# An RWKV-6 recurrence and a gated FFT convolution in one kernel: zero matmuls early on TensorE, the bonus added on VectorE, shared buffers, spectrum products slot by slot, and a new instruction order

## The chip, the cores and the metric

The kernel runs on one core of a Trainium2 chip. The metric is device time in microseconds of one execution, as the median of three runs. Engines are called as in the profile: PE is TensorE (PEld its weight loads), DVE is VectorE, ACT is ScalarE, POOL is GpSimd and SP is SyncE, which issues most of the DMAs.

## What is computed

Two layers. The first is a recurrence over 768 steps for 4 batches of 8 heads of 48 channels; the second projects the result three ways, convolves one projection along the sequence with a filter by FFT, multiplies by the other two and projects out.

```python
for t in range(S):
    cur = np.einsum('bhd,bhe->bhde', u[None] * kt, vt)
    y[:, :, t] = np.einsum('bhd,bhde->bhe', rt, state + cur)
    state = wt[:, :, :, None] * state + np.einsum('bhd,bhe->bhde', kt, vt)
...
x = attn_out.transpose(0, 2, 1, 3).reshape(B, S, H * D)
x1, x2, x3 = np.split(x @ w_proj, 3, axis=-1)
x2_conv = np.fft.irfft(np.fft.rfft(x2, axis=1) * np.fft.rfft(filter_fft, axis=0), axis=1)
return (x1 * x2_conv * x3) @ w_out
```

The term with `u` is the bonus: at each step it adds v times a number per head, the sum of r, k and u over the channels.

## The kernel before

**First layer.** The sequence of each batch is cut in 6 chunks of 128 steps, 24 chunks in all, numbered through the batches. A chunk is one set of [128 steps x 384 channels] tiles, and goes through these steps, whose names are those of the order table:

- `ldw ldk ldr ldv` (L384): four loads of 192 KB from a layout with 192-byte rows, each kind into a ring of 5 buffers.
- `lw` (ACT, L390) takes the logarithm of w; `cs`, `ce` (PE, L394 to L406) form its running sums; `en`, `eq`, `ph` (ACT, L412 to L424) their exponentials.
- `kh`, `q` (L430, L433) scale k and r by them, `rk`, `rku`, `cc` (L436 to L442) make the bonus number of each head, `v` (L231 to L233) casts v, and `vc` (L448) multiplies v by the bonus. They run on DVE or POOL, as the table says.
- `tqk` (PE, L454) transposes scaled k and r, `tT` copies them out of PSUM, `sc` (PE, L467) makes the scores, `mt` (DVE, L474) masks them, `kv` (PE, L483, L485) and `S` (DVE, L492) carry the state on.
- `y` (PE, L499 to L507) adds up in PSUM: vc through an identity matrix, then state times r, then scores times v. `xn` copies it out, `yt` (PE, L518) transposes it, `xT` copies that; for the second half of a batch `sa`, `sb` (DVE, L526, L529) form sums and differences with the first half.

**Second layer**, for each batch: `x2` (PE, L562) projects sums and differences, `ab` copies out; `f` (PE, L348, L356) is the forward transform in six slots of 128 rows, `X` copies out; `ua ub uc ud` (L584) multiply the spectrum by the filter's, `pr`, `pi` (L589, L593) combine the products; `iE`, `iO` (PE, L602) are the inverse transform in two halves for each of three column blocks, `ec`, `s`, `d` (L229 or L231, L617, L622) put them together. `p1`, `p3` (PE, L539) are the other two projections, `x1` copies one out, `g` (DVE, L555) multiplies them, `yy` (DVE, L627) multiplies by the convolution. `po` (PE, L634) projects out, `o` copies to a tile and `st` (L643) stores it. The filter's own spectrum (`fs fd hf H hg`) is made from one load, `ldfilt` (L307), and the transform matrices from sines (`ang`, `sin`, `m2t`, `m2c`).

**What sets the order.** A table of words written out by hand, `ORDER`, gives the order of the program. `V:ua.1.0` is: on DVE, ua of batch 1, piece 0; `P:y5@3` is: on PE, y of chunk 5, into PSUM bank 3. Each engine executes its own words in this order and waits in line for its inputs and buffers; nothing is reordered, on SP's DMA queue either. Six PSUM banks are shared by all steps and one wide tile is for the scores.

**What the steps of the prediction touch.** `GRAN = (3, 3, 3, 1)` says how many slots a spectrum product takes at once: in batches 0 to 2 one instruction covers all three pairs of slots (128x1152), in batch 3 there are three of 128x384. Tiles x1, ab, X, U and y exist once; the output tile exists twice, the second one in the filter's bytes. Before the table starts, PE runs 8 matmuls on a tile of zeros (`hot<-warm`, L687).

Of the kernel before, what the change touches and what calls it, by code (L numbers as in the profile page):

```python
# [12 lines left out]
INT32 = mybir.dt.int32  # L13
# [17 lines left out]
WARM = 8  # L31

# [4 lines left out]
A:tLn0 S:ldu G:masks S:ldw1 S:ldk0 S:ldw0 G:iota S:ldw2 S:ldk2 V:ang2 S:ldk1 V:ang0 S:ldw3  # L37
V:ang1 S:ldv1 A:lw2 A:lw0 P:cs2@0 P:ce2@1 S:ldr1 P:ce0@2 A:eq2 A:lw1 S:ldr0 P:ce1@3 P:cs1@4
P:cs0@5 A:eq1 S:ldr2 A:eq0 A:en1 S:ldv0 A:en0 V:kh1 A:ph2 A:lw3 G:kh0 A:en2 S:ldk3 A:v1 V:kh2
A:ph0 A:sin S:ldw5 V:q0 V:rk0 P:tqk0@4 S:ldw6 V:q1 G:q2 V:tT0 S:ldv2 V:rku0 G:v0 P:tqk2@5 V:cc0  # L40
P:cs3@1 S:ldr3 V:rk2 P:kv0@0 G:vc0 P:sc0@8 V:S0 P:ce3@2 V:mt0 S:ldw4 G:rku2 A:tT2 G:rk1 S:ldv3
V:cc2 P:y0@4 A:lw5 P:sc2@8 A:eq3 V:xn0 P:tqk1@0 A:en3 S:ldk4 V:rku1 G:v2 A:ph1 P:yt0@5 P:cs5@4
V:cc1 P:kv1@1 A:xT0 V:mt2 S:ldk6 A:lw6 G:rk3 A:ph3 A:tT1 S:ldr4 V:S1 G:vc2 A:lw4 V:vc1 P:kv2@3
A:en5 G:q3 S:ldv4 P:sc1@8 V:kh3 P:cs6@5 P:cs4@2 P:ce6@0 A:en4 G:rku3 P:y2@1 S:ldw8 V:S2 P:ce5@4
V:xn2 A:eq5 S:ldr5 G:v3 A:eq6 V:mt1 P:yt2@2 G:kh4 P:ce4@3 A:ph6 P:tqk3@1 S:ldr6 A:eq4 V:cc3
G:rk4 A:xT2 P:y1@4 V:tT3 S:ldk5 A:xn1 V:q4 G:rku4 P:sc3@8 P:m2t3@0 S:ldw7 P:m2t0@2 V:mt3
P:tqk4@1 P:yt1@4 A:tT4 S:ldr8 V:m2c3a G:q5 V:cc4 A:en6 V:vc3 P:m2t5@1 S:ldv7 P:sc4@8 A:xT1 G:rk6
# [88 lines left out]
def kernel(  # L136
# [307 lines left out]
    def op_v(e, c):  # L444
        copy(e, v_b[c % 4], ld["v"][c % 5])
# [274 lines left out]
```

## Time and profile before

| | |
|---|---|
| runs | 188.52 us median of 3 (187.33 to 189.53) |
| profiled execution | 188.97 us, span of its instructions 186.7 us |
| busy: PE, DVE, ACT, POOL | 154.7, 159.5, 117.3, 107.4 us |
| mean granted clock of PE | 0.962 |
| first logarithm starts | 7.92 us |
| filter load issued | 93.54 us |
| last input loads issued | 107.02 to 109.75 us |
| PE clock granted in 40 to 50 us | 0.65 |

The span is the time from the first to the last instruction of the profiled execution; the rest of its time lies around it. A row of a group names the line, the engine, the operation, output<-input with their shapes and the count, then busy time in all and the mean in ns of one, then the idle time of that engine just ahead of the group and what ended it. A row of a timeline starts with start and length in us. The rows of stages give start and length, then busy us and (count) of PE, PEld, DVE, ACT and POOL, the granted clock, the share of the DMA engines' time and GB/s.

### The profile page before, as it was taken

The page shows a single profiled execution, that of the slowest core. Times are in us where ns is not written, and L with a number is a line of the kernel's source. Part 1 is how long each engine was busy: PE and PEld are TensorE (multiplying, and loading weights), DVE is VectorE, ACT ScalarE, POOL GpSimd, SP SyncE. Part 2 cuts the span into 40 slices and gives each one's busy share as a digit, 9 for nine tenths or more (in the row PEclk, how much of TensorE's full clock was granted, in tenths as well). Part 3 has the DMA queues.
Part 4 walks back from the last instruction along what each step waited for, and adds up shares of the span by engine and source line. Part 5 has one row for each costly group of instructions (what it writes and reads, how often), then busy time and mean ns, then how long its engine had stood idle before and what let it go on. Part 6 is the DMA issues. An engine that isn't in the chain of part 4 may idle for free.

```text
span 186.7 us, 4118 instructions
## 1 busy us (share of the span) xinstructions
PE 154.7 (83%) x1526; PEld 97.8 (52%) x1526; DVE 159.5 (85%) x302; ACT 117.3 (63%) x257; POOL 107.4 (57%) x120
## 2 busy tenths in 40 slices
PE   5147787665799988897977799999999999999971
PEld 2115456444666546563655555756556655556630
DVE  6829989786989799989998979999998999699760
ACT  2289756976585497697486969988356415531532
POOL 6024899398651482995995636636651866781000
PEclk9999999995589999999999969999999999999999
DMA  4999999999999983999999890400001000335336
GB/s 104 202 219 201 192 188 205 199 177 197 193 195 188 213 172 76 196 191 214 176 248 241 172 203 5 63 4 0 0 4 42 0 0 4 126 125 214 130 144 235
DMA packets 105043, 26.41 MB, mean 141 GB/s; under 512 B 100288, under 2 KB 104640, under 8 KB 105024
## 3 DMA queue, kind: packets, MB, share of 16 engines
q1 hardware_dynamic: 104224, 24.98, 61.0%
q0 software_dynamic: 800, 1.18, 3.8%
q8 instruction: 12, 0.20, 0.4%
q14 instruction: 7, 0.06, 0.1%
HBM read 22.61 MB, written 4.72 MB: 146 GB/s over the span
## 4 chain that ended last, share of the span: by engine, by line
PE 56%; DVE 24%; ACT 9%; issue 4%; DMA 3%; SPq 2%; ACTq 0%
PE p L539 10%; PE po L634 6%; DVE mt L474 5%; PE iE L602 4%; PE iO L602 4%; PE f L356 4%; PE x L562 4%; ACT qkT L229 3%; PE tqk L454 3%; PE sc L467 3%; DVE cc L442 3%; PE y L507 2%; DVE S L492 2%; PE f L348 2%; DVE rku L439 2%
## 5 line engine op out<-in xcount | busy, mean ns | idle before, releaser
L539 PE MATMUL p<-xT,wproj 128*128 128x384 bf16 x144 | 30.0, 330 | 2.3 <-DVE S L492 2.0
L474 DVE TENSOR_TENSOR mt<-sc,mask_excl 128x1024 bf16<-128x1024 f32 x24 | 29.1, 1214 | 2.2 <-PE sc L467 2.2
L448 POOL TENSOR_TENSOR vc<-v,cc 128x384 bf16<-128x384 bf16 x19 | 16.8, 887 | 18.0 <-DVE cc L442 6.3
L430 POOL TENSOR_TENSOR qk<-ldk,en 128x384 bf16<-128x384 f32 x15 | 16.0, 1068 | 17.3 <-ACT phi L424 9.0
L436 POOL TENSOR_TENSOR rk<-ldr,ldk 128x384 bf16<-128x384 f32 x18 | 20.1, 1118 | 6.7 <-DVE rku L439 5.6
L229 ACT ACTIVATE qkT<-tqk 128x1024 bf16<-128x1024 bf16 x19 | 19.5, 1029 | 6.2 <-PE tqk L454 6.0
L454 PE MATMUL tqk<-ident,qk 128*128 128x128 bf16 x192 | 16.8, 238 | 5.0 <-POOL qk L430 2.1
L539 PEld LDWEIGHTS <-wproj 128*128 128x128 bf16 x144 | 13.0, 98 | 11.5 <-issue 4.4
L433 POOL TENSOR_TENSOR qk<-ldr,eq 128x384 bf16<-128x384 f32 x13 | 14.1, 1085 | 7.2 <-ACT eq L418 4.8
L229 ACT ACTIVATE x<-p 128x384 bf16<-128x384 f32 x20 | 9.6, 492 | 12.9 <-PE p L539 10.2
L454 PEld LDWEIGHTS <-qk 128*128 128x128 bf16 x192 | 13.2, 106 | 8.1 <-issue 4.0
L390 ACT ACTIVATE lg<-ldw 128x384 bf16<-128x384 f32 x24 | 12.7, 532 | 6.0 <-DMA ldw<-in_w_dram 5.9
L634 PE MATMUL po<-wout,y 128*128 128x384 bf16 x72 | 14.3, 326 | 1.3 <-DVE y L627 1.1
L412 ACT ACTIVATE en<-cs 128x384 f32<-128x384 f32 x24 | 11.7, 496 | 5.3 <-PE cs L394 5.2
L562 PE MATMUL x<-wproj,sd 128*128 128x384 bf16 x72 | 14.8, 326 | 0.0
L555 DVE TENSOR_TENSOR g<-p,x 128x384 bf16<-128x384 f32 x24 | 13.0, 549 | 1.8 <-PE p L539 1.8
L394 PE MATMUL cs<-lg,mask_incl 128*128 128x384 bf16 x24 | 9.5, 413 | 5.3 <-ACT lg L390 4.6
L418 ACT ACTIVATE eq<-ce 128x384 f32<-128x384 f32 x24 | 11.7, 495 | 3.1 <-PE ce L406 1.7
L492 DVE TENSOR_TENSOR S<-kv,phi 128x384 bf16<-128x384 f32 x20 | 11.0, 550 | 2.7 <-PE kv L485 2.2
L442 DVE TENSOR_REDUCE cc<-rku 128x8 f32<-128x384 bf16 x24 | 12.9, 541 | 0.1
L229 ACT ACTIVATE xn<-y 128x384 bf16<-128x384 f32 x17 | 8.4, 494 | 6.7 <-PE y L507 6.6
L602 PEld LDWEIGHTS <-P 128*128 128x128 bf16 x96 | 9.3, 98 | 6.1
(133 smaller groups left out, 410.2 us busy)
## 6 DMA issues: line engine op xcount, KB each, us to landing
ldw<-in_w_dram SPq DMA_DIRECT2D x24, 192.0 KB, 3.9
ldk<-in_k_dram SPq DMA_DIRECT2D x24, 192.0 KB, 3.8
ldv<-in_v_dram SPq DMA_DIRECT2D x24, 192.0 KB, 4.0
ldr<-in_r_dram SPq DMA_DIRECT2D x24, 192.0 KB, 3.9
out_dram<-o SPq DMA_DIRECT2D x12, 192.0 KB, 2.0
out_dram<-filt SPq DMA_DIRECT2D x12, 192.0 KB, 2.0
filt<-in_moe_filter_fft_dram SPq DMA_DIRECT2D x1, 1152.0 KB, 7.4
wproj<-in_moe_w_proj_dram POOLq DMA_DIRECT2D x1, 864.0 KB, 8.7
```

What stands on the lines that cost most here:

```text
L229: nc.scalar.activation(out=o, in_=i, func=AF.Copy)
L430: two(e).tensor_mul(qk_b[c % 3][:, 1, :, 0:D], ld["k"][c % 5], en_b[c % 3])
L436: two(e).tensor_mul(rk_b[c % 2], ld["r"][c % 5], ld["k"][c % 5])
L442: nc.vector.tensor_reduce(out=cc_b[c % 3], in_=rku_b[c % 2], axis=AX.X, op=ALU.add)
L448: two(e).tensor_mul(vc_b[c % 3], v_b[c % 4], cc_b[c % 3].to_broadcast([L, H, D]))
L454: nc.tensor.transpose(p[:, x, j, :], qk_b[c % 3][:, x, 2 * j:2 * j + 2, :], ident)
L474: nc.vector.tensor_mul(mt_b[c % 3], bank_of[f"sc{c}"].rearrange("p q j t -> p (q j) t"), dataclasses.replace(m[:, :], ap=[m[:, :].ap[0], [ ...
L492: nc.vector.tensor_mul(S_b[nth(c)], bank_of[f"kv{c}"], ph_b[nth(c)].to_broadcast([L, HP, 2, D]))
L539: nc.tensor.matmul(p, wproj[:, cb, col0:col0 + L], xT_b[b % 2][:, cb, sl], start=(cb == 0), stop=(cb == CB - 1),)
L562: nc.tensor.matmul(p, sd_b[q][0][:, cb, ti * L:(ti + 1) * L], wproj[:, cb, C:2 * C], start=(cb == 0), stop=(cb == CB - 1),)
L602: nc.tensor.matmul(p, P_b[q % 2][b % 2][:, q // 2, cb * L:(cb + 1) * L], m, start=(n == 0), stop=(n == len(slots) - 1),)
L634: nc.tensor.matmul(p, y_b[0][:, cb, ti * L:(ti + 1) * L], wout[:, cb, :], start=(cb == 0), stop=(cb == CB - 1),)
```

## The change

Five things, and all of them in one step.

1. **Zeros.** A word of PE can end in `+n`: then n matmuls of the zero tile go into the PSUM tile of that word just ahead of it. They write 384 columns at most, and the word's own first matmul overwrites them. The table has 78 in twelve places: 69 of them belong to chunks 0 to 5 (11 ahead of ce0, 6 ahead of tqk0, 11 ahead of y2, and so on), 9 stand ahead of the first output product of batch 3.
2. **Bonus.** y no longer gets vc through the identity matrix (24 matmuls fewer). `xn` becomes an addition of PSUM and vc, on DVE in all 24 chunks; before, it was a copy, 17 times on ACT and 7 times on DVE.
3. **Buffers.** Load rings go from 5 to 6, x1, ab, X and y from 1 to 2. The angles lie in the output tile's bytes, U in the filter's, the index map in E's; there is one output tile.
4. **Spectrum products** are 128x384 in all batches: `GRAN = (1, 1, 1, 1)`.
5. **Order.** The table is new as a whole: other places, banks and, where a step can run on several engines, other engines.

```diff
-    ld = {x: ring(f"ld{x}", 5, [L, H, D], FP32) for x in "wkrv"}
+    ld = {x: ring(f"ld{x}", 6, [L, H, D], FP32) for x in "wkrv"}
...
-    x1_b = ring("x1", 1, [L, CB, S], BF16)
+    x1_b = ring("x1", 2, [L, CB, S], BF16)
...
-    U_b = {m: ring(f"U{m}", 1, [L, 3, C], BF16) for m in "abcd"}
+    o_all = consts.tile([L, NCH, C], FP32)
+    filt = consts.tile([L, NCH, C], FP32)
+    ang = [
+        o_all.rearrange("p a c -> p (a c)")[:, t * S:(t + 1) * S].bitcast(INT32)
+        for t in range(NT)
+    ]
+    U_all = filt.rearrange("p a c -> p (a c)").bitcast(BF16).rearrange(
+        "p (m n c) -> p m n c", m=4, n=3
+    )
+    U_b = {m: U_all[:, i] for i, m in enumerate("abcd")}
...
     def ps(name, bank, shape=(L, C), dt=FP32):
...
+        wid = min(C, flat.shape[1])
+        for _ in range(warm_n[0]):
+            nc.tensor.matmul(
+                flat[:, 0:wid], warm[:, 0:L], warm[:, 0:wid], start=True, stop=True
+            )
         return t
...
     def op_y(e, c, bank):
...
+        if XADD:
+            for j in range(HP):
+                if ci > 0:
+                    state(j)
+                scores(2 * j, ci == 0, ci == 0)
+                scores(2 * j + 1, ci == 0, True)
+            return
         nc.tensor.matmul(p, ident, vc_b[c % 3], start=True, stop=False)
...
     def op_xn(e, c):
-        copy(e, xn_b[c % 3], bank_of[f"y{c}"].rearrange("p h d -> p (h d)"))
+        y = bank_of[f"y{c}"].rearrange("p h d -> p (h d)")
+        if XADD:
+            nc.vector.tensor_add(xn_b[c % 3], y, vc_b[c % 3].rearrange("p h d -> p (h d)"))
+        else:
+            copy(e, xn_b[c % 3], y)
...
-    GRAN = (3, 3, 3, 1)
+    GRAN = (1, 1, 1, 1)
```

Three places of the order, each before and in the change. The names are the program's tiles, with their buffer numbers.

**SP's first loads.** The tile ldw0 is w of chunk 0, and so on. Before:

```order
L302 DMA u_bc_165<-in_u_dram 128x384
L384 DMA ldw1_80<-in_w_dram 128x8x48
L384 DMA ldk0_84<-in_k_dram 128x8x48
L384 DMA ldw0_79<-in_w_dram 128x8x48
L384 DMA ldw2_81<-in_w_dram 128x8x48
L384 DMA ldk2_86<-in_k_dram 128x8x48
```

In the change:

```order
L330 DMA u_bc_170<-in_u_dram 128x384
L412 DMA ldw0_79<-in_w_dram 128x8x48
L412 DMA ldw1_80<-in_w_dram 128x8x48
L412 DMA ldk0_85<-in_k_dram 128x8x48
L412 DMA ldw3_82<-in_w_dram 128x8x48
L412 DMA ldr1_92<-in_r_dram 128x8x48
```

Before, ACT's first logarithm took w of chunk 2, the fifth DMA; now it takes w of chunk 0, the second. The filter's load moved from behind 85 loads to behind 21, and the weights' loads on POOL's queue moved ahead as well.

**DVE's spectrum products of batch 0.** X0 and X1 are the spectrum's two parts, HR, HI and HG the filter's; in the change U is named filt, whose bytes it has. Before they stand among steps of chunks 17 to 22:

```order
L584 TENSOR_TENSOR Uc0_156<-X0_0_148,HI_174 128x1152
L433 TENSOR_TENSOR qk1_103<-ldr2_91,eq1_109 128x8x48
L474 TENSOR_TENSOR mt2_133<-sc20_1993,mask_excl_184 128x1024
L492 TENSOR_TENSOR S2_136<-kv20_2012,phi2_113 128x384
L584 TENSOR_TENSOR Ub0_155<-X1_0_149,HI_174 128x1152
L526 TENSOR_TENSOR sd0_0_142<-xT0_140,yt17_2036 128x3x128
```

In the change, among those of chunks 6 to 8:

```order
L629 TENSOR_TENSOR filt_169<-X1_0_156,HI_177 128x384
L629 TENSOR_TENSOR filt_169<-X0_0_154,HI_177 128x384
L629 TENSOR_TENSOR filt_169<-X0_0_154,HR_176 128x384
L520 TENSOR_TENSOR S2_140<-kv6_984,phi2_117 128x384
L629 TENSOR_TENSOR filt_169<-X1_0_156,HI_177 128x384
L629 TENSOR_TENSOR filt_169<-X0_0_154,HR_176 128x384
L629 TENSOR_TENSOR filt_169<-X1_0_156,HG_178 128x384
L629 TENSOR_TENSOR filt_169<-X0_0_154,HI_177 128x384
L634 TENSOR_TENSOR P0_0_158<-filt_169 128x384
```

One instruction became three, and they moved ahead by eleven chunks. DVE has 64 products and sums of spectra now, 46 of them in batches 0 to 2, against 21 and 14 before; POOL has 8 against 15.

**DVE behind the sums of chunk 23**, the last chunk; yt23 is its transposed y. Before:

```order
L526 TENSOR_TENSOR sd0_0_142<-xT1_141,yt23_2428 128x3x128
L529 TENSOR_TENSOR sd1_0_143<-xT1_141,yt23_2428 128x3x128
L231 COPY o_167<-po_0_4_2432 128x384
L231 CAST ab0_147<-x2_3_1_1_2417 128x384
L617 TENSOR_TENSOR SD0_161<-iO_1_0_2438,E0_158 128x384
L555 TENSOR_TENSOR g0_145<-p3_2_0_0_2446,x10_144 128x384
```

In the change:

```order
L571 TENSOR_TENSOR sd0_0_146<-xT1_145,yt23_2709 128x3x128
L574 TENSOR_TENSOR sd1_0_147<-xT1_145,yt23_2709 128x3x128
L259 CAST ab1_153<-x2_3_0_2_2725 128x384
L259 COPY o_all_168<-po_2_5_2713 128x384
L600 TENSOR_TENSOR g1_151<-p3_3_1_0_2644,x11_149 128x384
L629 TENSOR_TENSOR filt_169<-X1_1_157,HI_177 128x384
```

Before, the rest of batch 1 and the inverse transforms of batches 2 and 3 follow; now only batch 3 is left, with two output copies of batch 2. DVE has 63 instructions from the first of these rows on before, and 39 now.

DVE's counts by step, before and in the change: kh 9 and 6, q 11 and 7, rk 6 and 8, rku 13 and 10, vc 5 and 0, v 5 and 2, tT 5 and 3, ab 6 and 1, X 4 and 0, x1 4 and 0, ec 7 and 0, xn 7 and 24, o 4 and 5, m2c 2 and 3, xT 3 and 2.

More of the change, by code (lines that the diff above doesn't have):

```diff
@@ L31 @@
 WARM = 8
+XADD = True
 ORDER = """
[L37 to L47, printed above, removed]
@@ L180 @@
     sd_b = [ring(f"sd{q}_", 1, [L, CB, HALF], BF16) for q in (0, 1)]
-    x1_b = ring("x1", 1, [L, CB, S], BF16)
+    x1_b = ring("x1", 2, [L, CB, S], BF16)
     g_b = ring("g", 2, [L, CB, S], BF16)
-    ab_b = ring("ab", 1, [L, 2, NT, C], BF16)
-    X_b = [ring(f"X{q}_", 1, [L, 3, C], BF16) for q in (0, 1)]
+    ab_b = ring("ab", 2, [L, 2, NT, C], BF16)
+    X_b = [ring(f"X{q}_", 2, [L, 3, C], BF16) for q in (0, 1)]
     P_b = [ring(f"P{q}_", 2, [L, 3, C], BF16) for q in (0, 1)]
-    U_b = {m: ring(f"U{m}", 1, [L, 3, C], BF16) for m in "abcd"}
-    E_b = ring("E", 3, [L, HALF], FP32)
+    E_all = consts.tile([L, 3, HALF], FP32)
+    E_b = [E_all[:, i, :] for i in range(3)]
     SD_b = ring("SD", 3, [L, 2, HALF], BF16)
-    y_b = ring("y", 1, [L, CB, S], BF16)
+    y_b = ring("y", 2, [L, CB, S], BF16)
+    o_all = consts.tile([L, NCH, C], FP32)
[8 more added lines that the diff above has]
+    U_b = {m: U_all[:, i] for i, m in enumerate("abcd")}
+    fmap = E_all[:, 0:2, :].rearrange("p a t -> p (a t)")
     u_bc = consts.tile([L, H, D], FP32)
-    filt = consts.tile([L, NCH, C], FP32)
-    o_b = [consts.tile([L, NCH, C], FP32, name="o"), filt]
     wproj = consts.tile([L, CB, 3 * C], BF16)
@@ L203 @@
     fd = consts.tile([L, NT, C], BF16)
-    fmap = consts.tile([L, S], FP32)
     tcol = consts.tile([L, NT], FP32)
     mpi = consts.tile([L, 1], FP32)
-    ang = ring("ang", NT, [L, S], INT32)
     mask_excl = consts.tile([L, L], BF16)
@@ L218 @@
     bank_of = {}
+    warm_n = [0]
     def ps(name, bank, shape=(L, C), dt=FP32):
@@ L384, in op_ld @@
         nc.sync.dma_start(
-            out=ld[x][c % 5],
+            out=ld[x][c % 6],
             in_=src[b, :, ci * L:ci * L + L, :].rearrange("h t d -> t h d"),
@@ L389, in op_lw @@
     def op_lw(e, c):
-        nc.scalar.activation(out=lg_b[c % 3][:, :, 0:D], in_=ld["w"][c % 5], func=AF.Ln)
+        nc.scalar.activation(out=lg_b[c % 3][:, :, 0:D], in_=ld["w"][c % 6], func=AF.Ln)
     def op_cs(e, c, bank):
@@ L444, in op_v @@
     def op_v(e, c):
-        copy(e, v_b[c % 4], ld["v"][c % 5])
+        copy(e, v_b[c % 4], ld["v"][c % 6])
     def op_vc(e, c):
@@ L498, in op_y, with state, scores @@
         p = ps(f"y{c}", bank, (L, H, D))
+        def state(j):
+            nc.tensor.matmul(
+                p[:, 2 * j:2 * j + 2, :], qkT_b[c % 3][:, 0, j, :],
+                S_b[nth(c - 1)][:, j], start=XADD, stop=False,
+            )
+        def scores(h, start, stop):
+            nc.tensor.matmul(
+                p[:, h, :], mt_b[c % 3][:, HP * (h % 2) + h // 2, :], v_b[c % 4][:, h, :],
+                start=start, stop=stop,
+            )
+        if XADD:
[5 more added lines that the diff above has]
+            return
         nc.tensor.matmul(p, ident, vc_b[c % 3], start=True, stop=False)
@@ L547, in op_x1 @@
     def op_x1(e, b, fb, hf):
-        copy(e, x1_b[0][:, fb, halves[hf]], bank_of[f"p1.{b}.{fb}.{hf}"])
+        copy(e, x1_b[b % 2][:, fb, halves[hf]], bank_of[f"p1.{b}.{fb}.{hf}"])
     def op_p3(e, b, fb, hf, bank):
@@ L581, in f @@
             sl = slice(n * GRAN[b], (n + 1) * GRAN[b])
-            x = X_b[0 if which in "ac" else 1][0][:, sl, :]
+            x = X_b[0 if which in "ac" else 1][b % 2][:, sl, :]
             h = dict(a=HR, b=HI, c=HI, d=HG)[which][:, sl, :]
-            two(e).tensor_mul(U_b[which][0][:, sl, :], x, h)
+            two(e).tensor_mul(U_b[which][:, sl, :], x, h)
         return f
@@ L639, in op_o @@
     def op_o(e, b, ti):
-        copy(e, o_b[b % 2][:, ti, :], bank_of[f"po.{b}.{ti}"])
+        copy(e, o_all[:, ti, :], bank_of[f"po.{b}.{ti}"])
     def op_st(e, b, ti):
-        nc.sync.dma_start(out=out[b, ti * L:(ti + 1) * L, :], in_=o_b[b % 2][:, ti, :])
+        nc.sync.dma_start(out=out[b, ti * L:(ti + 1) * L, :], in_=o_all[:, ti, :])
     table = {
@@ L652, in emit @@
         e, rest = word[0], word[2:]
+        rest, _, n = rest.partition("+")
+        warm_n[0] = int(n or 0)
         rest, _, bank = rest.partition("@")
```

221 lines of the change are left out of this document (118 added, 103 removed).

## The prediction

> **What bounds the kernel now.** I read the busy times first, then the table of four stages, the chain that ended last and the first start of the spectrum products.
>
> ```profile
> span 186.7 us, 4118 instructions
> PE 154.7 (83%) x1526; PEld 97.8 (52%) x1526; DVE 159.5 (85%) x302; ACT 117.3 (63%) x257; POOL 107.4 (57%) x120
> PE 56%; DVE 24%; ACT 9%; issue 4%; DMA 3%; SPq 2%; ACTq 0%
> 0.00:50.00 50.00, 31.21 (x328) 20.73 (x329) 39.46 (x81) 31.67 (x64) 32.37 (x48) 0.93 0.96 188
> 50.00:110.00 60.00, 51.94 (x621) 34.05 (x620) 55.85 (x95) 44.22 (x104) 38.41 (x41) 0.96 0.94 191
> 110.00:180.00 70.00, 68.75 (x566) 41.59 (x565) 63.59 (x127) 39.04 (x85) 36.59 (x32) 0.99 0.20 61
> 180.00:186.70 6.70, 2.83 (x17) 1.47 (x16) 0.56 (x1) 2.40 (x5) 0.00 (x0) 0.97 0.51 189
> L584 DVE TENSOR_TENSOR Ua<-X,HR x5: 349/682/759, 117.7 to 164.7; 128x1152 bf16<-128x1152 bf16 x3, 128x384 bf16<-128x384 bf16 x2
> ```
>
> The stage rows give start and length, then busy time (and count) of PE, PEld, DVE, ACT, POOL, then clock, DMA share and GB/s. Until 110 us DMA is nearly full, DVE works 95 of 110 us and PE only 83. After that DMA is nearly free and PE is solid (68.75 of 70): this is the backlog that the chain shows as PE 56%. The last row shows why it exists: no spectrum product starts before 117.7 us, since the filter is loaded late, so every inverse transform and output product lies behind that. DVE is idle 27.2 us in all: 10.5 up to 50 us, 4.1 up to 110, 6.4 up to 180, 6.1 at the end. PE has 32 us of slack. A better order can remove PE's backlog; then DVE, the busiest engine, sets the end. So I sum DVE's work and add the idle time that should stay.
>
> **The change part by part.** DVE's ledger comes from these rows:
>
> ```profile
> L231 DVE CAST xn<-y 128x384 bf16<-128x384 f32 x7 | 3.9, 553 | 3.3 <-PE y L507 3.3
> L584 DVE TENSOR_TENSOR Ub<-X,HI 128x1152 bf16<-128x1152 bf16 (+1 forms) x5 | 3.7, 743 | 0.0
> L584 DVE TENSOR_TENSOR Ua<-X,HR 128x1152 bf16<-128x1152 bf16 (+1 forms) x5 | 3.0, 592 | 0.1
> L584 DVE TENSOR_TENSOR Ud<-X,HG 128x1152 bf16<-128x1152 bf16 (+1 forms) x4 | 2.6, 651 | 0.0
> L584 DVE TENSOR_TENSOR Uc<-X,HI 128x1152 bf16<-128x1152 bf16 (+1 forms) x3 | 1.8, 610 | 0.0
> L589 DVE TENSOR_TENSOR P<-Ua,Ub 128x1152 bf16<-128x1152 bf16 (+1 forms) x3 | 1.8, 616 | 0.0
> L593 DVE TENSOR_TENSOR P<-Uc,Ud 128x1152 bf16<-128x1152 bf16 x1 | 0.8, 750 | 0.0
> L430 DVE TENSOR_TENSOR qk<-ldk,en 128x384 bf16<-128x384 f32 x9 | 6.3, 703 | 4.3 <-ACT en L412 4.3
> L433 DVE TENSOR_TENSOR qk<-ldr,eq 128x384 bf16<-128x384 f32 x11 | 7.1, 657 | 0.0
> L436 DVE TENSOR_TENSOR rk<-ldr,ldk 128x384 bf16<-128x384 f32 x6 | 5.1, 846 | 0.0
> L439 DVE TENSOR_TENSOR rku<-rk,u_bc 128x384 bf16<-128x384 bf16 x13 | 9.8, 751 | 0.1
> L448 DVE TENSOR_TENSOR vc<-v,cc 128x384 bf16<-128x384 bf16 x5 | 3.8, 766 | 0.0
> L231 DVE COPY qkT<-tqk 128x1024 bf16<-128x1024 bf16 x5 | 3.4, 678 | 0.0
> L231 DVE CAST v<-ldv 128x384 bf16<-128x384 f32 x5 | 3.3, 672 | 0.0
> L231 DVE CAST ab<-x 128x384 bf16<-128x384 f32 x6 | 3.2, 550 | 0.1
> L231 DVE CAST X<-f 128x384 bf16<-128x384 f32 x4 | 2.2, 548 | 0.1
> L231 DVE COPY E<-iE 128x384 f32<-128x384 f32 x7 | 3.8, 551 | 1.7 <-PE iE L602 1.6
> 158.48 0.35 DVE L584 TENSOR_TENSOR Ud<-X,HG 128x384 bf16<-128x384 bf16 x1
> 158.75 0.35 DVE L584 TENSOR_TENSOR Uc<-X,HI 128x384 bf16<-128x384 bf16 x1
> ```
>
> The last two stand in a queue: 0.35 us long but 0.27 apart, so each queued instruction costs 0.08 us less than its span. I take that off for every one added and removed.
>
> Spectrum products and their sums: 21 on DVE now, 13.7 us (3.7+3.0+2.6+1.8+1.8+0.8). After, 64 of 384 columns: 64 x 0.35 = 22.4, less 43 x 0.08, so +5.3 us. Bonus: all 24 of y's exits are DVE additions instead of 7 copies. An addition of a PSUM and an SBUF operand isn't shown for this tile; I take the copy's 0.553, so 17 x 0.553 - 17 x 0.08 = +8.0. The rest goes to other engines by the new order: kh 3 fewer (-2.1), q 4 (-2.6), rk 2 more (+1.7), rku 3 fewer (-2.3), vc 5 (-3.8), tT 2 (-1.4), v 3 (-2.0), ab 5 (-2.75), X and x1 4 each (-4.4), ec 7 (-3.9), and three single copies (+0.6): -22.95, and 37 instructions fewer give 3.0 back: -20.0. Together DVE changes by -6.7 us if nothing waits.
>
> **Waits at the split products.** 46 of the 64 belong to batches 0 to 2 and now run among POOL's chunk products.
>
> ```profile
> 159.24 0.91 POOL L593 TENSOR_TENSOR P<-Uc,Ud 128x384 bf16<-128x384 bf16 x1 [1.34 <-DVE Uc L584]
> 159.48 0.88 DVE L584 TENSOR_TENSOR Ub<-X,HI 128x384 bf16<-128x384 bf16 x1
> L430 DVE TENSOR_TENSOR qk<-ldk,en x9: 540/549/1268, 12.3 to 126.3; 128x384 bf16<-128x384 f32 x9
> L627 DVE TENSOR_TENSOR y<-SD,g x12: 543/550/559, 137.8 to 179.3; 128x768 bf16<-128x768 bf16 x12
> ```
>
> Started during a POOL product, a DVE product took 0.88 us instead of 0.35: 0.53 lost. The five kinds with both operands in SBUF (kh, q, rk, rku, vc) have the undisturbed 0.54 as minimum and means of 0.657 to 0.846: (means - 0.54) x counts is 8.4 us over 44, 0.19 each. The final products yy (last row), with both operands in SBUF too, never waited. So the cost is 0 to 46 x 0.19 = 8.7 us. The split products sit where kh and q do, which speaks for 0.19, but often stand in runs of three or more, in which mainly the first can meet POOL; I take 0.13, 6.0 us. DVE's work is then 159.5 - 6.7 + 6.0 = 158.8, between 152.8 and 161.5: nearly no change. The Trainium skill ("SBUF — State Buffer", Who interferes with whom) says that a VectorE instruction with two SBUF inputs and a GpSimd one that reads SBUF exclude each other, the second waiting out the first. The 0.88 row agrees; it is a rule against this change, and what it would do here is the first rival.
>
> **PE.** 24 bonus matmuls go, 78 zero ones come, at the pace of the po row below (0.174 us each): -4.2 and +13.6 us. Of the zeros 69 stand in the first 50 us, 12 us into 18.8 of idle time, and nine at the end, while PE waits for DVE. I cost both at nothing on the path; where a group of 11 is not covered it holds up 1.9 us. The xn additions now wait for POOL's vc, with all of DVE queued behind; before, y's first matmul waited for it:
>
> ```profile
> L499 PE MATMUL y<-vc,ident 128*128 128x384 bf16 x24 | 8.5, 354 | 2.9 <-DVE S L492 1.3 <-POOL vc L448 1.0 <-ACT qkT L229 0.6
> ```
>
> That was 1.0 us in all and is needed twelve matmuls later now: nothing to 1.0, taken as nothing. Shared bytes (angles in the output tile, U in the filter's) tie only work that lies far apart in the new order: nothing, likewise the sixth load buffer. The filter's 1.18 MB at 188 GB/s pushes early loads back 6 us; by 50 us 42 loads can still be in, and DVE's work up to there uses about 36. From nothing to 3 us; nothing taken.
>
> **The start and the tail.**
>
> ```profile
> 1.11 2.74 PE L687 MATMUL hot<-warm 128*128 128x384 bf16 x8 [1.11 <-DVE warm L669]
> 7.92 0.94 ACT L390 ACTIVATE lg<-ldw 128x384 bf16<-128x384 f32 x2 [5.91 <-DMA ldw<-in_w_dram]
> 12.31 0.56 DVE L430 TENSOR_TENSOR qk<-ldk,en 128x384 bf16<-128x384 f32 x1 [3.61 <-ACT en L412]
> 147.07 0.35 DVE L526 TENSOR_TENSOR sd<-xT,yt 128x384 bf16<-128x384 bf16 x1
> 179.90 2.95 PE po L634 x17
> 182.87 0.49 ACT filt L229
> ```
>
> The first logarithm needs the second load now, not the fifth, and chunk 0 goes alone. 8 + 11 zeros at 2.74/8 = 0.34 us hold PE until 1.1 + 6.5 = 7.6; two products and an exponential later kh0 starts near 9 instead of 12.31. I take 3 us off the 10.5 of early idle: 7.5. From 50 us to the last chunk's sums I keep the DVE idle share of 50 to 110 us, 4.15/60 = 6.9%, since DVE leads there as it will now.
>
> Behind the sums of chunk 23 (147.07 us, 39.6 before the end) DVE has 63 instructions now and 39 after: all but two belong to batch 3. Their spans add up to 17.4 us, less 39 x 0.08: 14.3. As a chain: sums and last x2 1.2, ab 0.55, six transforms of 0.52 3.1, X 0.5: 5.4. Eighteen products and three g run beside it from about 3 and end at 3 + 18 x 0.27 + 3 x 0.47 = 9.3; three pairs of inverses at 1.4 and s, d, yy bring 13.5; six po 3.1 and o 0.5: 17.1; from 183.4 (last o) to 186.7 another 3.3: 20.5 us.
>
> **Sum.** DVE's work before those sums is 158.8 - 14.3 = 144.5. They end at t with t = 144.5 + 7.5 + 0.069 (t - 50): t = 159.6. With the tail the span is 180.1. Around the span this execution had 188.97 - 186.7 = 2.3 us, so 182.4 against 188.97; the median of the runs, 188.52, lies 0.45 lower, so 182.0.
>
> **Rivals.** *POOL holds DVE* (slower). All 46 meet POOL in proportion to its 64% in 50 to 110 us and lose the 0.53 of the one measured meeting: 0.34 each, 15.6 us instead of 6.0. DVE is the bound, so +9.6/0.931 = 10.3: 192.3 us. It turns slower than 190.4 from 0.30 each. For it: the 0.88 row, and runs of products that hold POOL back in turn. Against it: the mean of 0.19 in the busiest stages. By the rule of the Trainium skill ("SBUF — State Buffer", Who interferes with whom) alone it comes out so wherever the two overlap.
>
> *The idle time moves instead of going* (no change). With PE and DVE both near full, each product between them waits once: at 12% idle in the middle t = (144.5 + 7.5 - 6)/0.88 = 165.9, span 186.4, 188.2 us. For it: 9% DVE idle while PE led. Against it: 6.9% while DVE led and loads were the limit.
>
> *Nothing waits* (faster still). No loss at the products and 5% idle: t = (138.5 + 7.5 - 2.5)/0.95 = 151.1, 173.5 us.
>
> **How the numbers follow.** Forecast 0.53, nothing waits 0.20, idle moves 0.13, POOL holds DVE 0.14. About 1% is what a measurement of this kernel can tell: below 186.6 is faster, above 190.4 slower. Faster 0.73, within 1% 0.13, slower 0.14. The range 174 to 190 takes in the bounds of the waits (-6.0/+2.7), the filter (3) and most of the no-change case.
>
> **What would show it.** Right: no PE stretch of 60 us at full; first spectrum product before 65 us; DVE busy within 156 to 162 us; split products at 0.45 to 0.5 us mean; kh0 near 9 us; sums of chunk 23 near 160 us and some 20 us behind them. Wrong: split products at 0.6 or more; DVE idle over 10% between 50 and 150 us; PE's clock falling in the middle, where the zeros don't stand.

## The result and the profile after

The changed kernel takes 171.79 us (median of 4 runs, 171.63 to 172.81) against 187.93 us for the kernel before (median of 4 runs, 185.15 to 189.53). That is 16 us faster, where 6.5 were forecast, and below the low end of the range. The ratio is 0.9235, with a 95% interval from 0.9125 to 0.9346; it and all ratios and times of the experiments are of a kernel's fast runs alone, those within 1.5% of its fastest, which for before are 185.15 and 187.33 us here, so that this ratio stands for some 14 us. In the rounds of the experiments before had medians of 187.3 to 188.0 us, again some 16 us above the change. The profiled execution took 171.63 us. From its page the head, PE's clock and the chain, then three stages, cut at 50 us and at 147.9 us, where the sums of chunk 23 start:

```profile
span 169.9 us, 4263 instructions
PE 153.3 (90%) x1580; PEld 96.9 (57%) x1580; DVE 155.1 (91%) x325; ACT 122.6 (72%) x272; POOL 100.9 (59%) x118
PEclk9998799999999998589999999999999999999999
PE 71%; DVE 19%; ACT 5%; issue 2%; DVEq 0%
```

```profile
0.00:50.00 50.00, 42.86 (x446) 26.82 (x446) 44.52 (x101) 34.33 (x72) 29.32 (x43) 0.97 0.98 200
50.00:147.90 97.90, 92.38 (x1024) 60.03 (x1023) 95.37 (x186) 78.37 (x179) 71.59 (x76) 0.97 0.68 141
147.90:169.90 22.00, 18.05 (x114) 10.01 (x112) 15.20 (x40) 9.88 (x22) 0.00 (x0) 0.99 0.32 117
```

Between 50 and 148 us PE and DVE are both nearly full: DVE 95.37 and PE 92.38 of 97.90 us. Before, DVE was idle 10.5 us of the first 50 and PE 18.8; now it is 5.5 and 7.1. The clock row has a dip near 65 to 75 us, which leads to the one thing that nobody ordered. DVE's rows come first, then POOL's:

```profile
62.56 0.35 DVE L638 TENSOR_TENSOR P<-filt 128x384 bf16<-128x384 bf16 x1
62.83 5.15 DVE L458 TENSOR_TENSOR qk<-ldk,en 128x384 bf16<-128x384 f32 x1
67.90 0.55 DVE L556 TENSOR_TENSOR xn<-y,vc 128x384 bf16<-128x384 f32 x1
```

```profile
62.10 0.80 POOL L345 DMA_DIRECT2D wout<-in_moe_w_out_dram  x1
62.93 0.92 POOL L634 TENSOR_TENSOR P<-filt 128x384 bf16<-128x384 bf16 x1
63.80 1.94 POOL L461 TENSOR_TENSOR qk<-ldr,eq 128x384 bf16<-128x384 f32 x2
65.70 0.91 POOL L467 TENSOR_TENSOR rku<-rk,u_bc 128x384 bf16<-128x384 bf16 x1
66.58 0.98 POOL L464 TENSOR_TENSOR rk<-ldr,ldk 128x384 bf16<-128x384 f32 x1
```

The product kh of chunk 11, 0.55 us elsewhere, takes 5.15 us on DVE. It begins while POOL is issuing the load of the output weights, and it ends 0.4 us behind the last of the five products that POOL runs right after that issue; a sixth has begun by then, after a pause of 0.08 us. The sum P ahead of it, of two SBUF operands too, begins in the middle of the issue and takes its undisturbed 0.35 us, so the issue alone doesn't hold DVE. So 4.6 us of DVE's "busy" time are a wait. PE pays for it too:

```profile
62.00:68.00 6.00, 2.07 (x40) 1.41 (x40) 6.00 (x5) 1.52 (x5) 5.90 (x8) 0.91 1.08 186
68.00:72.00 4.00, 3.50 (x16) 1.98 (x17) 4.00 (x8) 2.18 (x5) 0.75 (x1) 0.50 1.00 196
68.50 0.50 PE L563 MATMUL yt<-ident,xn 128*128 128x128 bf16 x3 [4.43 <-DVE xn L556]
```

PE is busy 2.07 of 6 us behind the stall and idle for 4.43 us in one piece, and its clock is granted at 0.50 from 68 to 72 us. The Trainium skill ("TensorE: Matmul & The Clock Gate", Part 1) says that the clock falls to half after an idle window of about 3.4 us; these rows agree. In the tenth kernel below it falls as well, without an idle stretch of that length.

### The profile page after: what moved, and what is told of

Its sections match the earlier page's. It is cut to its first block, busy times and chain, and to the rows that moved or that the text cites. A ratio compares the mean times of both kernels' runs of the same rounds, so it can differ in the third digit from the quotient of the medians.

```text
span 169.9 us, 4263 instructions
## 1 busy us (share of the span) xinstructions
PE 153.3 (90%) x1580; PEld 96.9 (57%) x1580; DVE 155.1 (91%) x325; ACT 122.6 (72%) x272; POOL 100.9 (59%) x118
## 4 chain that ended last, share of the span: by engine, by line
PE 71%; DVE 19%; ACT 5%; issue 2%; DVEq 0%
PE p L584 12%; PE po L679 7%; PE x L607 6%; PE iO L647 5%; PE tqk L482 5%; PE f L384 4%; DVE mt L502 4%; DVE qk L458 3%; PE iE L647 3%; PE sc L495 3%; PE f L376 3%; PE yt L563 3%; PE y L534 3%; PE cs L250 2%; PE ce L428 2%
## 5 line engine op out<-in xcount | busy, mean ns | idle before, releaser
L458 POOL TENSOR_TENSOR qk<-ldk,en 128x384 bf16<-128x384 f32 x18 | 19.1, 1062 | 18.5 <-DMA ldk<-in_k_dram 7.0
L476 POOL TENSOR_TENSOR vc<-v,cc 128x384 bf16<-128x384 bf16 x24 | 20.8, 872 | 9.9 <-DVE cc L470 4.1
L257 ACT ACTIVATE xT<-yt 128x384 bf16<-128x384 bf16 x22 | 10.9, 494 | 14.4 <-PE yt L563 12.1
L461 POOL TENSOR_TENSOR qk<-ldr,eq 128x384 bf16<-128x384 f32 x17 | 17.7, 1045 | 5.1 <-ACT phi L452 3.2
L464 POOL TENSOR_TENSOR rk<-ldr,ldk 128x384 bf16<-128x384 f32 x16 | 17.8, 1117 | 2.5 <-DMA ldr<-in_r_dram 1.8
L467 POOL TENSOR_TENSOR rku<-rk,u_bc 128x384 bf16<-128x384 bf16 x14 | 13.2, 946 | 4.3 <-DVE rk L464 4.2
L257 ACT ACTIVATE x<-p 128x384 bf16<-128x384 f32 x24 | 11.8, 504 | 3.2 <-PE p L584 3.2
L556 DVE TENSOR_TENSOR xn<-y,vc 128x384 bf16<-128x384 f32 x24 | 13.0, 548 | 0.8 <-PE y L534 0.5
L257 ACT ACTIVATE X<-f 128x384 bf16<-128x384 f32 x24 | 11.7, 498 | 1.8 <-PE f L384 1.4
L257 ACT ACTIVATE o_all<-po 128x384 f32<-128x384 f32 x19 | 9.3, 503 | 5.1 <-PE po L679 5.0
```

The lines of the kernel that those rows point to most:

```text
L257: nc.scalar.activation(out=o, in_=i, func=AF.Copy)
L458: two(e).tensor_mul(qk_b[c % 3][:, 1, :, 0:D], ld["k"][c % 6], en_b[c % 3])
L461: two(e).tensor_mul(qk_b[c % 3][:, 0, :, 0:D], ld["r"][c % 6], eq_b[c % 3])
L464: two(e).tensor_mul(rk_b[c % 2], ld["r"][c % 6], ld["k"][c % 6])
L467: two(e).tensor_mul(rku_b[c % 2], rk_b[c % 2], u_bc)
L476: two(e).tensor_mul(vc_b[c % 3], v_b[c % 4], cc_b[c % 3].to_broadcast([L, H, D]))
```

## The experiments

Fifteen kernels, three rounds each against the kernel before. All times are medians in us, with the ratio to before and its 95% interval; the changed kernels are compared with one another by their times. Theory: the new order with the products in pieces fills PE and DVE at once, and both set the end. Rival, as in the forecast: DVE alone sets it.

**Zeros and bonus taken away.** The first removes the zeros, the second gives the bonus back to PE. In the second, four of 24 chunks (3, 9, 20, 22) have vc behind y in the table, so their y gets an older chunk's vc.

```diff
-P:ce0@0+11 ... P:ce1@2+4 ...
+P:ce0@0 ... P:ce1@2 ...
```

> The changed kernel without its 78 zero matmuls, all else the same. If the zeros only fill idle time and the gain is the order's: 171 to 173 us, as with them (171.8). If they bring a part of the gain by holding PE's clock up: the clock falls below 0.8 in some 10 us of the first 50, DVE waits for PE there, and the time is 174 to 177.

```diff
-XADD = True
+XADD = False
```

> The changed kernel with the bonus back in PSUM by 24 identity matmuls; xn stays on DVE, as a copy. PE gets 24 x 0.17 = 4.1 us more, DVE the same. If DVE sets the end: 171.5 to 173. If PE does (the chain puts 71% on it): 175 to 176.5.

Without zeros 173.34 (0.9202, 0.9148 to 0.9256), 1.5 us slower than the change, between the two ranges that I had given; the runs of the two kernels overlap (172.25 to 173.41 and 171.63 to 172.81). With the bonus on PE 175.34 (0.9330, 0.9280 to 0.9381), 3.5 us slower for 24 matmuls that I had put at 4.2 us, as expected if PE sets the end. The forecast had these matmuls at nothing on the path. Not all of the 3.5 need be matmul work: in the second kernel PE also waits 2.6 us in all for POOL's vc at y, which it doesn't in the changed one.

**The stall: where the output weights' load is issued.** Third: the issue goes behind kh of chunk 12, still in a busy row of POOL. Fourth: the issue stays, but kh of chunk 11 goes to POOL and a sum (pr) to DVE in its place.

```diff
-A:lw12 G:ldwo P:y8@1
+A:lw12 P:y8@1
...
-V:cc10 G:kh12 A:ph13
+V:cc10 G:kh12 G:ldwo A:ph13
```

> In the changed kernel one DVE product (kh of chunk 11, at 62.8 us) takes 5.15 us instead of 0.55, beside POOL's issue of the wout load and five POOL products in a row. Here only that load's issue moves, behind kh of chunk 12 on POOL. If a DMA issue on POOL is what blocks DVE: kh of chunk 11 takes under 1.2 us, and the time falls to 167 to 169. If the row of POOL products keeps the port from DVE: it stays at 4 to 5 us, and the time at 171 to 173.

```diff
-V:kh11 G:pr.0.2
+G:kh11 V:pr.0.2
```

> Two instructions change engines: kh of chunk 11 goes to POOL, the sum pr of batch 0, slot 2, to DVE, so no DVE product starts beside the wout issue and the row of POOL products. DVE's work is the same but for the stall of 4.6 us. By both theories of the stall, and if DVE sets the end: 167 to 169 us. If PE sets the end: 171 to 172, since PE's idle time just moves.

Third: 168.04 (0.8928, 0.8874 to 0.8981). The same kh now takes 1.27 us, and a shorter stall has moved along with the issue; POOL's rows, then DVE's:

```profile
69.38 0.81 POOL L339 DMA_DIRECT2D wout<-in_moe_w_out_dram  x1
70.21 1.63 POOL L470 TENSOR_TENSOR vc<-v,cc 128x384 bf16<-128x384 bf16 x2
71.79 0.99 POOL L458 TENSOR_TENSOR rk<-ldr,ldk 128x384 bf16<-128x384 f32 x1
70.40 2.80 DVE L666 TENSOR_TENSOR y<-SD,g 128x768 bf16<-128x768 bf16 x1
```

Fourth: 173.29 (0.9185, 0.9109 to 0.9260). It missed its 167 to 169: with kh gone, the product next to the issue is caught. POOL, then DVE:

```profile
63.24 0.80 POOL L339 DMA_DIRECT2D wout<-in_moe_w_out_dram  x1
62.99 6.01 DVE L623 TENSOR_TENSOR filt<-X,HI 128x384 bf16<-128x384 bf16 x2
```

So it isn't that product, but the issue with what follows it on POOL. What was still open: would POOL's five products do it without an issue ahead of them? The eighth kernel leaves the five where they are and issues the load near 44 us, where POOL has nothing to do behind it. (The expectations that follow write 166.8 us for this kernel, the median of its four runs.)

```diff
-G:q7 P:x2.0.0.1@3
+G:q7 G:ldwo P:x2.0.0.1@3
...
-A:lw12 G:ldwo P:y8@1
+A:lw12 P:y8@1
```

> The changed kernel with POOL's issue of the output weights' load moved from 62 us to a place behind q of chunk 7, near 44 us, where POOL then waits about 3 us for v of chunk 6. Theory (a DMA issue on POOL with a row of POOL products right behind it shuts DVE's two-SBUF products out until the row ends): the 5.15 us product of chunk 11 falls below 1.3 us, no DVE product of two SBUF operands takes over 1.5 us, 166 to 168 us. Rival (the five POOL products in a row at 62.9 us do it by themselves): the product of chunk 11 still takes 4 us or more, and the time stays at 171 to 172 us. Second rival (the load itself, wherever it stands, costs its 4.6 us): a stall of over 2 us near 45 us and 170 to 172 us.

165.00 (0.8771, 0.8696 to 0.8847): the fastest kernel here that leaves out no work. POOL, then DVE:

```profile
43.92 0.80 POOL L339 DMA_DIRECT2D wout<-in_moe_w_out_dram  x1
47.33 1.07 POOL L470 TENSOR_TENSOR vc<-v,cc 128x384 bf16<-128x384 bf16 x1 [2.61 <-DVE v L253]
...
62.82 0.96 POOL L628 TENSOR_TENSOR P<-filt 128x384 bf16<-128x384 bf16 x1 [0.56 <-DVE filt L623]
63.74 2.26 POOL L455 TENSOR_TENSOR qk<-ldr,eq 128x384 bf16<-128x384 f32 x2
```

```profile
62.93 1.26 DVE L452 TENSOR_TENSOR qk<-ldk,en 128x384 bf16<-128x384 f32 x1
```

The same DVE product stands beside the same row of POOL products and takes 1.26 us: it gets in after one of them. So the issue with a row of POOL products right behind it is what shuts DVE out until the row pauses. One difference is left: kh begins 0.10 us ahead of the row's first product in the changed kernel and 0.11 us behind it here. It doesn't decide, since yy of the third kernel begins 0.19 us behind its row's first product and is shut out all the same. The issue without a row costs little or nothing: before, it was followed at 116.58 us by 1.7 us without a POOL product, and a DVE product of two SBUF operands that began 0.3 us behind it took its undisturbed 0.68 us. Two more of the kernels below have the same pair of DVE products beside the issue. In the sixth (first row) POOL runs nothing for 0.6 us behind the issue, in the twelfth (second row) one product at once:

```profile
60.76 1.58 DVE L620 TENSOR_TENSOR filt<-X,HI 128x1152 bf16<-128x1152 bf16 x2
61.76 2.69 DVE L620 TENSOR_TENSOR filt<-X,HI 128x1152 bf16<-128x1152 bf16 x2
```

So the wait grows with the row: about 1.1 us for one product, 2.3 for three, 4.6 for five. Why a row behind an issue is not shared, as it is without one, stays open.

The Trainium skill ("SBUF — State Buffer", Who interferes with whom) says that a VectorE instruction with two SBUF inputs and a GpSimd one that reads SBUF exclude each other. The trace agrees in that every product that stalled (kh, filt, yy) has both inputs in SBUF; that a whole row gets ahead of the waiting instruction, the page does not say.

**Buffers back to one, products back to whole pieces, order alone.** Fifth: x1, ab, X and y single, rings of five. In the order as it stands two of 24 output tiles (tiles 1 and 4 of batch 2) then read a third of y that belongs to batch 3. Sixth: whole products, each at the place of its last piece, the inverses that stood ahead of it behind it. Seventh: both of these, without zeros and with the bonus on PE.

```diff
-    x1_b = ring("x1", 2, [L, CB, S], BF16)
+    x1_b = ring("x1", 1, [L, CB, S], BF16)
```

> The changed kernel with x1, ab, X and y back to one buffer for each tile and five load buffers instead of six; order, zeros, bonus and split products stay. Theory (the gain comes from the order, which fills PE and DVE together; the buffers are not what it needs): 171.8 to 174 us, and the waits of ACT and DVE for the tiles ab, x1, X and y add less than 2 us on the engines that bound. Rival (the new order interleaves batches and needs the second buffers to do it): 176 us or more, with PE idle 5 us longer between 50 and 150 us.

```diff
-    GRAN = (1, 1, 1, 1)
+    GRAN = (3, 3, 3, 1)
```

> The changed kernel with batches 0 to 2 multiplied in whole pieces of 1152 columns again (each at the place of the last of its three pieces; the inverses that stood before it go behind it): 48 products and sums in place of 18 + 30 fewer. DVE's work falls by some 3 us (a product of 1152 columns took 0.68 undisturbed, three of 384 take 1.05 less 0.16 for the queue). Theory (PE and DVE are both full, DVE's work counts about half): 170 to 172 us. Rival (the pieces let the inverses start early and PE starves without them): 174 us or more, with PE's busy time in 50 to 70 us lower by 2 us or more.

> Only the new order (and the shared bytes) of the change: no zeros, the bonus on PE, one buffer for each of x1, ab, X and y, five load buffers, whole products in batches 0 to 2. In four of the 24 chunks the order has the bonus product behind the matmul that reads it, so that matmul takes an older chunk's value. Theory (the order brings the gain): 175 to 178 us, that is 171.8 plus the 1.5 and 3.5 us that the first two experiments showed for zeros and bonus, plus or minus 1 for the rest. Rival (the order pays only together with buffers and pieces): 183 us or more.

Fifth: 171.27 (0.9139, 0.9058 to 0.9219), as the change itself: the buffers carry nothing that shows. Sixth: 186.41 (0.9919, 0.9842 to 0.9995), where I had expected 170 to 172: the theory that saved DVE work would be worth half of itself fell, and the rival holds by its time. Its sign, 2 us less of PE in 50 to 70 us, shows only against the eighth kernel (14.61 against 18.93 us), since the changed one (15.05) has its stall there. Seventh: 189.07 (1.0051, 0.9958 to 1.0145): the new order without pieces gains nothing. In the sixth, PE waits for POOL's whole sums (2.4 to 2.9 us each), which could have been the cause by itself. So, after that:

**Pieces without the order, whole products on DVE alone, and one batch.** Eleventh: the order of before, products of batches 0 to 2 in pieces at their old places. Twelfth: the sixth kernel with all products of batches 0 to 2 on DVE. Fifteenth: as the twelfth, but batch 0 alone whole.

```diff
-V:ua.0.0
+V:ua.0.0 V:ua.0.1 V:ua.0.2
```

> The kernel before with only one part of the change: the spectrum products and sums of batches 0 to 2 slot by slot, each trio at the place of the whole one. Theory (pieces pay only where the order puts them as their transforms come in): 188 to 192 us, as DVE and POOL get 36 more instructions at places where nothing earlier can start. Rival (pieces alone let the inverses start early): 184 us or less.

```diff
-G:pr.0.0 ... G:ub.1.0 ... G:pi.1.0 ... G:pr.2.0 G:pi.2.0
+V:pr.0.0 ... V:ub.1.0 ... V:pi.1.0 ... V:pr.2.0 V:pi.2.0
```

> The changed kernel with whole products in batches 0 to 2 as in the sixth experiment (187.1 us), but all of them on DVE: the five that POOL had there took 2.4 to 2.9 us each and PE waited 7.3 us for their sums. Theory (the loss was POOL's long products in front of the inverses): 172 to 178 us. Rival (the loss is that whole products come only after the last of six transforms, whichever engine does them, and everything queued behind on PE and DVE waits with the inverses): 181 us or more.

```diff
-    GRAN = (1, 1, 1, 1)
+    GRAN = (3, 1, 1, 1)
```

> The changed kernel with whole products on DVE in batch 0 alone (in all of batches 0 to 2 it was 186.4 us). Theory (each batch's late products hold up PE by some 5 us): 175 to 178 us. Rival (the first batch sets all that follows): 182 us or more. Second rival (a single late batch is absorbed, the loss needs the batches to push one another): 171 to 173.5 us.

Pieces in the old order: 192.72 (1.0206, 1.0142 to 1.0270), slower by some 2%. Whole products on DVE: 186.36 (0.9893, 0.9851 to 0.9936), so POOL's long products were not the cause. In the twelfth kernel PE's waits show the lateness, and PE's clock falls behind it:

```profile
66.31 0.82 PE L638 MATMUL iE<-m,P 128*128 128x384 bf16 x2 [3.58 <-DVE P L625]
...
143.89 0.40 PE L486 MATMUL sc<-qkT 48*128 48x128 bf16 x8 [2.73 <-DVE mt L493]
```

```profile
50.00:70.00 20.00, 14.72 (x145) 8.43 (x143) 14.45 (x21) 11.94 (x28) 10.35 (x10) 0.83 1.05 199
```

The first inverse transform is due 3.6 us before its whole product is there; all that stands behind it on PE, and then on DVE, waits along. In the eighth kernel, which has no stall in it, that stretch has 18.93 us of PE and 20.00 of DVE. Batch 0 alone whole: 172.39 (0.9227, 0.9131 to 0.9323). By its time that is the second rival, "absorbed", but this kernel has the same first wait (3.6 us) and no 5-us stall, since POOL has one product behind its issue there instead of five:

```profile
61.44 0.80 POOL L338 DMA_DIRECT2D wout<-in_moe_w_out_dram  x1
62.27 1.00 POOL L454 TENSOR_TENSOR qk<-ldr,eq 128x384 bf16<-128x384 f32 x1
70.98 1.00 POOL L454 TENSOR_TENSOR qk<-ldr,eq 128x384 bf16<-128x384 f32 x1 [7.71 <-ACT phi L445]
```

Against the eighth kernel, which has no stall either, it is 7.4 us slower, and the twelfth with three whole batches is 21.4 us slower, 7.1 a batch. So each late batch does seem to cost its share, more than the 5 us that I had put. That comparison was drawn afterwards, so I count it as argued. Nor is it shown that another order could not make whole products pay.

**Which engine sets the end.** Both start from the eighth kernel. Ninth: from chunk 8 on only half of the mask product is done. Tenth: in batches 1 and 2 two of three projection matmuls are left out.

```diff
+        hn = H if c < 8 else H // 2
...
+        last = 1 if b in (1, 2) else CB
```

> The version with the output weights' load issued early (166.8 us), with half of the mask product mt left out in chunks 8 to 23: DVE does 16 times some 0.55 us less, 8.8 us, and PE's work is untouched. Theory (PE and DVE are both full, so neither alone sets the end): 163 to 166 us, a gain of at most 4 us, with DVE's idle time growing by 5 us or more. Rival, the forecast's own argument (DVE, the busiest engine, sets the end): 157 to 159 us. Second rival (PE alone sets it): 166 us or more.

> The same version, mt whole, with two of three projection matmuls left out in batches 1 and 2: 48 matmuls of 0.174 us, 8.4 us less for PE, DVE's work untouched. Theory (both full): 163 to 166 us, PE's idle time up by 5 us or more. Rival (DVE sets the end, PE costs nothing): 166 to 167 us. Second rival (PE alone sets the end, as the 3.5 us for 4.2 us of bonus matmuls suggest): 158 to 160 us.

DVE lighter: 164.36 (0.8735, 0.8691 to 0.8779), 0.6 us faster than the eighth kernel, which is within its interval. PE lighter: 167.15 (0.8902, 0.8855 to 0.8948), some 2 us slower than the eighth, and the two intervals don't overlap. "DVE sets the end" asked for 157 to 159 in the ninth and "PE alone" for 158 to 160 in the tenth; neither came. My own 163 to 166 holds the ninth's time and misses the tenth's.

The ninth is a weaker test than planned. The mask products take 8.6 us less, but DVE's busy time falls by only 4.1 us, from 151.1 to 147.0, since other products of two SBUF operands take longer instead (above all q, 0.825 us in the mean against 0.585 in the eighth). DVE's idle time grows by 2.9 us, not by the 5 that I had expected. Even so, 4.1 us at full worth would have made 160.9. PE is full in 70 to 90 and in 110 to 130 us (20.00 of 20 us), as it is in the eighth kernel. The tenth shows how saved PE work goes lost:

```profile
70.00:74.00 4.00, 2.12 (x23) 1.25 (x24) 4.00 (x9) 2.70 (x7) 3.92 (x4) 0.83 1.09 216
74.00:78.00 4.00, 4.00 (x20) 1.89 (x15) 3.78 (x7) 2.36 (x6) 1.77 (x2) 0.50 1.04 204
78.00:80.00 2.00, 2.00 (x10) 1.02 (x9) 0.00 (x0) 1.55 (x5) 0.29 (x1) 0.62 1.15 220
```

With less to do, PE is idle for half of 4 us, its longest idle stretch being 1.24 us; its clock goes to 0.50, and DVE then stands still for 2.5 us, waiting for kv. In the eighth kernel the same 10 us have PE full at a clock of 1.00.

**Do the parts add up, and are the zeros' 1.5 us their own?** Thirteenth: the change without zeros and with the bonus on PE. Fourteenth: the eighth kernel without zeros.

> The changed kernel without zeros and with the bonus on PE: order, pieces and buffers of the change stay (four of 24 chunks take an older chunk's bonus value). Theory (the parts add): 171.8 + 1.5 + 3.5 = 176.8, so 176 to 178 us; order with pieces then brings some 11 of the 16 us. Rival (zeros only matter where PE has less work, bonus matmuls keep it as busy): 174 to 175.5 us. Second rival (zeros and bonus need each other): 179 us or more.

> The version with the output weights' load issued early (166.8 us), without the zeros. Theory (the zeros' 1.5 us is their own, from an earlier warm start of the first 50 us): 168 to 169.5 us. Rival (they only helped around the stall): 166 to 167.3 us.

176.61 (0.9452, 0.9371 to 0.9533), against 176.8 by adding: the parts add. 168.72 (0.9029, 0.8962 to 0.9097), 3.7 us slower than the eighth (2.4 us by the spans of the profiled executions): the zeros bring their gain without the stall too. So, in the changed kernel, order with pieces brings some 11 of the 16 us, the bonus 3.5, the zeros 1.5.

## Why the prediction was wrong

The direction held, and so did the undisturbed durations on DVE; the waiting around them was sized too large, and PE's part was costed at nothing. By the terms of its sum:

| term | forecast | measured |
|---|---|---|
| DVE's work before the sums of chunk 23 | 144.5 | 44.52 + 95.37 = 139.9 |
| of it the stall of kh | 0 | 4.6 |
| early idle of DVE | 7.5 | 5.5 |
| idle from 50 us to the sums | 0.069 x 109.6 = 7.6 | 97.90 - 95.37 = 2.5 |
| the sums start | 159.6 | 147.9 |
| tail behind them | 20.5 | 22.0 |
| span | 180.1 | 169.9 |

**The step that failed first** is "From 50 us to the last chunk's sums I keep the DVE idle share of 50 to 110 us, 4.15/60 = 6.9%, since DVE leads there as it will now": 2.6% was measured, which is 5.0 us less. The reason given, that loads were the limit, does not bear it. The eighth kernel keeps DMA as full in 70 to 90 us with DVE at 20.00 of 20:

```profile
70.00:90.00 20.00, 20.00 (x231) 13.21 (x229) 20.00 (x42) 19.20 (x45) 16.80 (x17) 1.00 1.03 204
```

What decides the idle time is whether PE and DVE find their next inputs ready, and that came with the pieces in the new order: with whole products on DVE, the idle time in 50 to 70 us alone is 5.6 us.

**The second failed step** is "I take 0.13" for a wait at a split product, with the old mean durations of kh, q, rk and rku kept beside it. These groups of after:

```profile
L629 DVE TENSOR_TENSOR filt<-X,HI 128x384 bf16<-128x384 bf16 x22 | 7.7, 370 | 0.5 <-ACT X L257 0.5
L629 DVE TENSOR_TENSOR filt<-X,HG 128x384 bf16<-128x384 bf16 x12 | 5.3, 450 | 0.0
L629 DVE TENSOR_TENSOR filt<-X,HR 128x384 bf16<-128x384 bf16 x11 | 4.7, 428 | 0.1
L634 DVE TENSOR_TENSOR P<-filt 128x384 bf16<-128x384 bf16 x10 | 3.6, 373 | 0.0
L638 DVE TENSOR_TENSOR P<-filt 128x384 bf16<-128x384 bf16 x9 | 4.0, 451 | 0.0
L467 DVE TENSOR_TENSOR rku<-rk,u_bc 128x384 bf16<-128x384 bf16 x10 | 5.7, 567 | 0.1
L464 DVE TENSOR_TENSOR rk<-ldr,ldk 128x384 bf16<-128x384 f32 x8 | 4.6, 573 | 0.0
L461 DVE TENSOR_TENSOR qk<-ldr,eq 128x384 bf16<-128x384 f32 x7 | 4.0, 564 | 0.1
```

By their means, the 64 products and sums of spectra take 26.0 us: 0.407 each, 0.057 lost over all 64, where 28.4 us (64 x 0.35 + 6.0) were in the sum; 2.4 us less. rku, rk and q take 14.2 us where the old means made 18.9, 4.7 less, and kh and v another 1.5 less without the stall. That is 8.6 us of waits that weren't there. The unforeseen stall of 4.6 took about half of them back, which leaves 4.0 of the table's 4.6 us; the rest I did not trace.

**PE at nothing on the path** was the third: the bonus taken off PE, with its waits for vc, was worth 3.5 us, and the zeros on PE brought 1.5 us, where both stood at nothing. Lightening DVE by itself was worth 0.6 us and lightening PE by itself nothing, so neither engine sets the end alone. That the two set it together fits these runs but is argued. The forecast's mark for this, "no 60-us PE stretch at full", is plainly false in the profile after: PE is busy 92.42 of the 93 us from 72 to 165 us, longer than before, with DVE busy 87.39 of them.

**Right:** the xn addition at 0.548 us (taken: 0.553) and the undisturbed product at 0.35; the first spectrum product at 50.1 us (forecast: before 65); kh0 at 7.62 (near 9); the tail within 1.5 us. Two of the signs for "right" were missed on the fast side: DVE's busy 155.1 us (156 to 162) and the split products' mean of 0.407 (0.45 to 0.5). The rivals on the slow side fell. "Nothing waits", 173.5 us, was the nearest, and in its terms too (5% idle, no loss). PE's clock did fall in the middle, which was named as a sign of error, but for a cause that no rival had.

## What to carry to other kernels

When two engines are both near full, do not carry the idle share of the old order into the new one: ask at each hand-over whether the input will be there, since that is what an order with finer pieces changes, and cost both engines' work on the path, not only that of the busiest. A DMA issue on POOL belongs where POOL pauses behind it, not ahead of a row of products. Splitting an instruction and moving it can each be worth nothing or less alone and bring most of the gain together.

## What the runs showed of the hardware that was not expected

The stall above: 4.6 us for a DVE product of two SBUF operands beside a POOL DMA issue with five products behind it, 2.3 us with three behind it in the third kernel, some 1.1 us with one in the twelfth, and little or none where POOL was idle behind the issue.

And the clock row can read full while PE is slow. The state matmul of the same chunk without the zeros (fourteenth kernel), then with them (eighth):

```profile
18.58 0.53 PE L505 MATMUL kv<-S,ident 128*128 128x384 bf16 x1
```

```profile
19.65 0.33 PE L505 MATMUL kv<-S,ident 128*128 128x384 bf16 x1
```

The clock row of the fourteenth kernel reads 1.00 in every slice of the early stage, yet from 18 to 33 us its matmuls of 384 columns take 0.50 to 0.53 us, instead of 0.33 in the eighth. In two of the fourteenth's four executions the mean granted clock is 0.918 instead of 1.00, at about the same times (168.37 and 169.25 against 168.47 and 168.98 us). So the slow stretch seems to be there in all four, and the clock record to show it in two; only one execution has a trace, so this isn't shown. As an estimate, 0.918 over 166.6 us would be 27 us at half clock.

In 20 to 30 us DVE does 7.71 us of work instead of 9.68, and its first sums of half a batch come at 39.4 us instead of 36.9. These 2.5 us are about the 2.4 by which the two spans differ (166.2 and 163.8 us). In this trace what the zeros do is seen in the duration of the matmuls, not in the clock row.
